# Linear attention, MoE and a second MLP on one core: the attention units from 10 on in one TensorE visit each, their k transposed on VectorE and through DRAM

## The chip, the core and the metric

One core of one Trainium2 chip runs the whole program. The metric is the device time of one execution in microseconds. The kernel before takes 721.27 us, the median of 3 runs (721.01 to 721.33). The engines are called by the names of the profile: PE is TensorE's matmuls and PEld its weight loads, DVE is VectorE, ACT is ScalarE, POOL is GpSimd, and SP is the engine whose queue issues nearly all DMAs.

## What is computed

Three layers, one after the other, on 3072 tokens (4 batches x 768) of 8 heads x 48 channels:

```python
for t in range(S):                       # attention, state [B, H, D, D], D = 48
    cur = einsum('bhd,bhe->bhde', u * k[t], v[t])
    y[:, :, t] = einsum('bhd,bhde->bhe', r[t], state + cur)
    state = w[t][..., None] * state + einsum('bhd,bhe->bhde', k[t], v[t])
x = y as [3072, 384]
h = x @ w_in                             # first MLP, 384 -> 2048 -> 384
x = (h * sigmoid(1.702 * h)) @ w_out
h = x @ w2_in                            # second MLP, 384 -> 1024 -> 384
s = h * softmax(h)
out = (s - mean(s)) / sqrt(var(s) + 1e-6) * g_ln @ w2_out
```

All is float32; the products of the MLPs are made of three matmuls each, on a high and a low part of either factor.

## The kernel before

**Units and blocks.** The tokens are cut into 24 attention units of 128 tokens (NU), each of two chunks of 64. The first MLP takes them in eight blocks of units, `BLOCKS`: three blocks of 2 units, two of 3 (blocks 3 and 4), three of 4 (blocks 5 to 7). A block runs in 16 steps, one for each 128 columns of the hidden layer. A step is `hstep` (line 597): `rise` (554), nine matmuls of the first layer into a PSUM bank `h` of which there are two; `gelu` (564), two ScalarE operations; and `rest` (572), one VectorE subtraction that makes the low part (the "gelu difference" below). `drain` (604) then runs `fall` (578), nine matmuls of the second layer, for the step two before. The columns of a matmul are the tokens of the block: 384 in blocks 3 and 4, 512 in blocks 5 and 6. After a block's last `fall`, `store` (590) copies the sums on ScalarE.

**Attention beside it.** While block j runs, the units of block j+1 are computed in the gaps. Up to about unit 9 the order of all engines is a list written out by hand, `START` (line 40). From unit 9 on, beside blocks 3 to 6, `steps_of` (716) says which of a unit's parts follow which step. Every engine runs its instructions in program order, and so does SP its DMAs: a DMA that waits holds all that stand behind it.

A unit i needs, on the way from load to output:
- `load_rkw` (105): r, k and the decay w by channel, 112 rows (48 channels of chunk 1, a gap, 48 channels of chunk 0), two buffers; `load_nat` (113): r and k by token; `load_v` (120) and `load_v2` (129).
- `f_scan` (135, forward products of w, VectorE), `f_r1` (141, GpSimd) and `f_r0` (147, VectorE), `f_back` (153: a small ScalarE copy `pc`, a reciprocal and the backward scan, line 159), `f_k` (162, the k product, line 166). They make scaled r and k.
- `bonus` (177, two GpSimd products), `bonus_sum` (184), `bonus_mul` (195, two GpSimd products of 64 rows, line 205), which leave the u term in `vd`.
- TensorE: `turn_k` (213, four transposes of k, line 217) with `copy_k` on ScalarE (219); `scores` (224, 16 small matmuls, lines 240 to 243 for units from 6 on), masked on VectorE (245, line 252); `states` (255, 16 small matmuls, lines 265 to 268), with `update` on VectorE (290, lines 305 and 308); `mix` (310, 32 small matmuls, lines 327 and 328), which makes y.
- `total` (330, adds y and `vd`), `send` (339, a 32x32-block transpose on VectorE and a DMA to DRAM), `fetch` (346, four DMAs back, so that y is transposed) and `out_hi`, `out_lo` (364, 374), which write the MLP's input.

**Visits.** In `steps_of` a unit is two visits of TensorE: `one` (727) has the transposes and scores of unit i+1 and the mix of unit i; `two` (758) has the states of unit i+1. Between them lie other steps. In a block of 3 units the visits follow steps 1, 6, 11 and 4, 9, 14; in one of 4 they follow steps 0, 4, 8, 12 and 2, 6, 10, 14. So units 9 to 11 run beside block 3, 12 to 15 beside block 4, 16 to 19 beside block 5 and 20 to 23 beside block 6. Where a block of 3 is followed by one of 4, the last unit (15) is `short`: its output goes through TensorE transposes (`turn`, 354, line 358) instead of DRAM.

**Queues.** On SP a unit's order is: rkw of unit i+3, v of i+2, the y write, four y reads (which wait for the write), v2, r and k by token.

Of the kernel before, what the change touches and what calls it, by code (L numbers as in the profile page):

```python
# [15 lines left out]
H, D, C = 8, 48, 64  # L16
HD = H * D
HC = H * C
# [5 lines left out]

QUADS = UB
DFF2 = NF2 * 128

# [39 lines left out]


def heads(ap, n=C):
    return ap.rearrange("p (h t) -> p h t", h=H)  # L70


class Attention:
# [31 lines left out]
    def load_rkw(self, i):  # L105
        if i < NU:
            rkw = self.get(i)["rkw"] = self.ap.tile([112, 2 * HC + H * PW + 2], F32, tag="rkw", name=f"rkw{i}", bufs=2)
            cut = 2 * HC if i < 2 else 0
            self.nc.sync.dma_start(out=rkw[:, cut:], in_=self.rkw[i, :, cut:])
            if cut:  # L110
                self.nc.sync.dma_start(out=rkw[:, 0:cut], in_=self.rkw[i, :, 0:cut])

# [55 lines left out]

    def front(self, i):
        if i < NU:  # L170
            self.f_scan(i)
            self.f_r1(i)
            self.f_r0(i)
            self.f_back(i)
            self.f_k(i)

    def bonus(self, i):
# [16 lines left out]

    def bonus_mul(self, i, e=None):
        nc, ap, s = self.nc, self.ap, self.st[i]
        dg = s["dg"]
        if e is not None:
            for h in range(H):
                v = s["vd"][:, h * D:(h + 1) * D]  # L200
                nc.scalar.activation(out=v, in_=v, func=AF.Copy, scale=dg[:, h:h + 1])
# [6 lines left out]
    def bonus_v(self, i):  # L208
        if i < NU:
            self.bonus_sum(i)  # L210
            self.bonus_mul(i)

# [42 lines left out]
    def states(self, i, chunk=None):  # L255
# [34 lines left out]
    def update(self, i, b, e=None):  # L290
# [7 lines left out]

        kv = self.bank(i, 3)[q:q + 48].rearrange("p (b c) -> p b c", b=2)[:, :, 0:4 * D]
        if b:  # L300
# [29 lines left out]
    def total(self, i, e=None):  # L330
        y, vd = self.st[i]["y"], self.st[i]["vd"]
        if i >= QUADS:
            vd = vd.rearrange("p (b c) -> p b c", b=2)
# [54 lines left out]
def rwkv_moe_moe2(ctx: ExitStack, tc: tile.TileContext, rkw, nat, vn, v2n, cst, w1, w2i, w2o, gln, out):  # L388
# [324 lines left out]
    at.dram = ctx.enter_context(tc.tile_pool(name="yd", bufs=2, space=bass.MemoryType.DRAM))  # L713
    at.spare = [x2b[:, (4 + k) * HD:(5 + k) * HD] for k in range(3)]

    def steps_of(j):

        S = [[] for _ in range(NF1)]  # L720
        u0, n = BLOCKS[j + 1]
        ones, twos = ((0, 4, 8, 12), (2, 6, 10, 14)) if n == 4 else ((1, 6, 11), (4, 9, 14))
        for i, a, b in zip(range(u0, u0 + n), ones, twos):
            nx, nn = i + 1 < NU, i + 2 < NU
            short = i + 1 == u0 + n and BLOCKS[j][1] < n

            def one(i=i, nx=nx, short=short):
                if nx:
                    at.turn_k(i + 1)
                    at.copy_k(i + 1)  # L730
                    at.scores(i + 1)
                at.mix(i)
                if nx:
                    at.load_rkw(i + 3)
                at.load_v(i + 2)
                at.total(i)
                if not short:
                    at.send(i)
                    at.fetch(i)
                if nx:  # L740
                    at.masked(i + 1, 0)
                    at.masked(i + 1, 1)

            def scan(i=i):
                at.f_scan(i + 2)
                at.f_r1(i + 2)

            def back(i=i):
                at.f_back(i + 2)

            def sums(i=i):
                at.bonus_sum(i + 1)

            def give(i=i):
                at.out_hi(i, X)
                at.out_lo(i, X)

            def two(i=i, nx=nx, short=short):
                if short:
                    at.turn(i)  # L760
                if nx:
                    at.states(i + 1)
                    at.load_v2(i + 2)
                if short:
                    give(i)
                if nx:
                    at.update(i + 1, 0)
                    at.update(i + 1, 1)
                    at.bonus_mul(i + 1)
                    at.load_nat(i + 3)  # L770
                    at.bonus(i + 2)

            def rest_of(i=i):
                at.f_k(i + 2)
                at.f_r0(i + 2)

            S[a] += [one]
            if nn:
                S[a + 1] += [scan]
            if nx:  # L780
                S[a if n == 4 else b - 1] += [sums]
            if nn:
                S[a + (1 if n == 4 else 2)] += [back]
            S[b] += [two]
            if not short:
                S[a + 3 if n == 4 else a + 4] += [give]
            if nn:
                S[b + 1] += [rest_of]
        return S

# [25 lines left out]
    with tc.manual_schedule():  # L816
        pend += [(2, NF1 - 2), (2, NF1 - 1)]
        for j in range(3, LAST):
# [116 lines left out]
def _layout(inp):  # L935
# [9 lines left out]

    rkw = np.zeros((NU, 112, 2 * HC + H * PW + 2), f)
# [6 lines left out]
    rkw[:, :, 2 * HC:-2] = wv.reshape(NU, 112, H * PW)  # L953

# [43 lines left out]
```

## Time and profile before

| | |
|---|---|
| median of 3 runs | 721.27 us (721.01 to 721.33) |
| profiled execution | 719.98 us, span 718.2 us |
| TensorE busy | 696.4 us (97%), clock granted 1.00 |
| VectorE busy | 548.2 us (76%) |
| ScalarE busy | 301.9 us (42%) |
| GpSimd busy | 167.0 us (23%) |
| blocks 3 to 6 | about 172 to 436 us of the span |

The span is what the profiler saw from the first to the last instruction; the execution's time is a little longer. A busy TensorE is read from starts: matmuls overlap, so the distance from one step's first matmul to the next step's is the step's cost. A group's idle time names what released it.

### The profile page before, as it was taken

Reading aid. Unit: us, or ns where it says so; the run is one execution under the profiler, and the core shown is the slowest. Engines: PE = TensorE matmul, PEld = TensorE weight load, DVE = VectorE, ACT = ScalarE, POOL = GpSimd, SP = SyncE. Lnnn points to the kernel's source line nnn. Section 1 sums busy time; section 2 is a strip of 40 time slices with the busy share of each in tenths; the row PEclk is TensorE's granted clock in tenths of the full one; section 3 lists DMA queues with packets and bytes.
Section 4 is the critical chain, followed back from the end, with each engine's and each line's share of the span. In section 5 each row is a group of like instructions: output and inputs, shape, how many; then the busy total and the mean of one; then the engine's idle time right before and its main releaser. Section 6 shows DMA issues by size and latency. Waiting matters only on the chain.

```text
span 718.2 us, 16290 instructions
## 1 busy us (share of the span) xinstructions
PE 696.4 (97%) x6596; PEld 619.3 (86%) x6596; DVE 548.2 (76%) x884; ACT 301.9 (42%) x604; POOL 167.0 (23%) x158
## 2 busy tenths in 40 slices
PE   2899999999999999999999999999999999999997
PEld 2679999999999999888888888888889989999997
DVE  8899999887767888866777632578588887788872
ACT  1465554333322322333223322465656545454552
POOL 5341222443333333423333300120000000000000
PEclk9999999999999999999999999999999999999999
DMA  8866624433333443333332103233135445444543
GB/s 252 271 189 216 219 80 113 120 100 89 104 95 97 127 128 97 95 95 100 101 91 56 34 23 103 80 103 89 59 117 180 152 140 180 144 140 144 161 155 103
DMA packets 53611, 88.77 MB, mean 124 GB/s; under 512 B 13632, under 2 KB 43200, under 8 KB 53536
## 3 DMA queue, kind: packets, MB, share of 16 engines
q1 hardware_dynamic: 53392, 87.63, 40.9%
q8 instruction: 52, 0.85, 0.5%
q14 instruction: 23, 0.19, 0.1%
q10 hardware_dynamic: 144, 0.10, 0.0%
HBM read 67.65 MB, written 20.05 MB: 122 GB/s over the span
## 4 chain that ended last, share of the span: by engine, by line
PE 92%; DVE 4%; ACT 2%; issue 1%; DMA 0%; ACTq 0%; DVEq 0%
PE acc L585 28%; PE h L560 26%; PE o L696 13%; PE right L628 8%; PE left L628 6%; PE att L327 2%; PE att L240 1%; PE att L217 1%; DVE P L138 1%; PE att L265 1%; PE att L328 1%; PE d L482 1%; DVE R L150 1%; PE att L358 1%; PE att L233 0%
## 5 line engine op out<-in xcount | busy, mean ns | idle before, releaser
L585 PE MATMUL acc<-gh,w 128*128 128x256 f32 (+2 forms) x768 | 212.4, 342 | 1.1 <-ACT x2a L595 0.8
L560 PE MATMUL h<-xTh,w 128*128 128x256 f32 (+2 forms) x768 | 173.9, 337 | 0.1
L568 ACT ACTIVATE gh<-h 128x256 fp32r<-128x256 f32 (+2 forms) x128 | 62.9, 491 | 244.5 <-PE h L560 236.2
L585 PEld LDWEIGHTS acc<-gh,w 128*128 128x128 f32 x768 | 136.5, 189 | 14.3 <-ACT x2a L595 1.1
L575 DVE TENSOR_TENSOR gl<-h,gh 128x256 fp32r<-128x256 f32 (+2 forms) x128 | 70.5, 553 | 90.2 <-ACT h L570 89.1
L560 PEld LDWEIGHTS h<-xTh,w 128*128 128x128 f32 x768 | 128.4, 189 | 12.3 <-ACT w L484 0.5
L585 PE MATMUL acc<-gl,w 128*128 128x256 f32 (+2 forms) x384 | 129.0, 336 | 0.0
L560 PE MATMUL h<-xTl,w 128*128 128x256 f32 (+2 forms) x384 | 87.6, 336 | 0.0
L585 PEld LDWEIGHTS acc<-gl,w 128*128 128x128 f32 x384 | 72.7, 189 | 5.3
L144 POOL TENSOR_TENSOR R<-rkw,P 64x512 f32<-64x512 f32 x24 | 32.1, 1336 | 185.3 <-issue 136.7
L696 PE MATMUL o<-w,qh 128*128 128x384 f32 x384 | 70.9, 336 | 0.0
L560 PEld LDWEIGHTS h<-xTl,w 128*128 128x128 f32 x384 | 64.7, 189 | 5.9 <-DVE xTl L378 0.2
L696 PEld LDWEIGHTS o<-w,qh 128*128 128x128 f32 x384 | 67.7, 188 | 1.6
L205 POOL TENSOR_TENSOR vd<-vs,dg 64x384 f32<-64x384 f32 x48 | 54.5, 1135 | 40.9 <-DVE dg L188 17.9
L570 ACT ACTIVATE h<-h 128x256 f32<-128x256 f32 (+2 forms) x128 | 62.5, 488 | 0.0
L673 POOL TENSOR_TENSOR sm<-sm,mhalf 128x1 f32<-128x1 f32 x24 | 13.2, 549 | 200.4 <-DVE sm L672 187.2
L159 DVE TENSOR_TENSOR_SCAN rkw<-rkw,ipc 112x520 f32<-112x520 f32 x24 | 41.6, 1731 | 0.8
L628 PE MATMUL right<-w,x2h 128*128 128x512 f32 x156 | 40.0, 392 | 0.9 <-ACT x2h L616 0.9
L181 POOL TENSOR_TENSOR nr<-nr,nk 128x384 f32<-128x384 f32 x24 | 27.7, 1155 | 43.3 <-DMA nk<-in_nat 42.1
L252 DVE TENSOR_TENSOR R<-att,cc 64x256 f32<-64x256 f32 (+1 forms) x82 | 36.7, 448 | 1.1
L696 PE MATMUL o<-w,ql 128*128 128x384 f32 x192 | 37.1, 334 | 0.0
L628 PEld LDWEIGHTS right<-w,x2h 128*128 128x128 f32 x156 | 29.1, 188 | 6.8 <-ACT x2h L616 1.2
(188 smaller groups left out, 1199.2 us busy)
## 6 DMA issues: line engine op xcount, KB each, us to landing
rkw<-in_rkw SPq DMA_DIRECT2D x22, 676.4 KB, 5.8
d<-t SPq DMA_DIRECT2D x24, 512.0 KB, 2.6
back<-d SPq DMA_DIRECT2D x96, 128.0 KB, 2.9
x2b<-in_w SPq DMA_DIRECT2D x11, 768.0 KB, 5.3
nr<-in_nat SPq DMA_DIRECT2D x24, 192.0 KB, 3.4
nk<-in_nat SPq DMA_DIRECT2D x24, 192.0 KB, 2.5
vs<-in_vn SPq DMA_DIRECT2D x48, 96.0 KB, 5.1
out<-ob SPq DMA_DIRECT2D x23, 192.0 KB, 2.2
```

The costliest lines, as they stand in the source:

```text
L144: (e or self.nc.gpsimd).tensor_tensor(out=heads(R1[0:64]), in0=heads(s["rkw"][0:64, 0:HC]), in1=heads(s["P"])[0:64, :, 0:C], op=ALU.mult)
L159: v.tensor_tensor_scan(out=w[:, n:0:-1], data0=w[:, n:0:-1], data1=self.ipc[:, n:0:-1], initial=0.0, op0=ALU.mult, op1=ALU.add)
L181: g.tensor_tensor(out=s["nr"], in0=s["nr"], in1=s["nk"], op=ALU.mult)
L205: nc.gpsimd.tensor_tensor(out=heads(vd[q:q + 64]), in0=heads(vt[q:q + 64]), in1=dg[q:q + 64].unsqueeze(2).to_broadcast([64, H, D]), op=ALU ...
L252: self.nc.vector.tensor_tensor(out=heads(R[q:q + 64])[:, h:h + n], in0=a, in1=m.unsqueeze(1).to_broadcast([64, n, C]), op=ALU.mult)
L560: nc.tensor.matmul(out=h_ps, lhsT=W1[f][:, ws + c * 128:ws + (c + 1) * 128], rhs=xs[:, c, tok], start=n == 0, stop=n == 8)
L568: nc.scalar.activation(out=gh, in_=h_ps, func=AF.Gelu_apprx_sigmoid)
L570: return nc.scalar.activation(out=h_ps, in_=h_ps, func=AF.Gelu_apprx_sigmoid)
L575: nc.vector.tensor_tensor(out=gl_, in0=g, in1=gh.bitcast(F32), op=ALU.subtract)
L585: nc.tensor.matmul(out=a, lhsT=W1[f][:, ws + e * 128:ws + (e + 1) * 128], rhs=gs, start=first and n == 0, stop=last and n == 2)
L628: nc.tensor.matmul(out=h_ps[:, b * 512:(b + 1) * 512], lhsT=xs[:, c], rhs=W2I[c][wb][:, b * 512:(b + 1) * 512], start=n == 0 and c == 0, s ...
L696: nc.tensor.matmul(out=o, lhsT=(lo if n == 2 else hi)[:, f * 128:(f + 1) * 128], rhs=W2O[f][n == 1], start=n == 0 and f == 0, stop=n == 2 ...
```

## The change

Units from `LONE` = 10 on are handled by a new table. `VISITS` gives the steps (counted from the start of block 3) after which units 9 to 23 have their one visit: 1, 6, 10, 14, 18, 22, 26, then every fourth from 32 to 60. Seven units (9 to 15) fall beside blocks 3 and 4, as before, but in other places. The lines of `ENTRY`, `SHORT` and `LONG` say what follows a visit's step, the next step, and so on; "+1" is the unit after the visit's.

- A visit holds scores and states of unit i+1 and the mix of unit i. For that, states go to the second half of their banks, and y to the bank that the transposed k had.
- k is no longer transposed on TensorE for units 11 to 23. `send_k` transposes it in 32x32 blocks on VectorE, writes it to DRAM and reads it back with four DMAs; `place_k` copies it on ScalarE, in two operations, where `copy_k` put it. For that the rkw load of these units has 128 rows, of which 16 are zero.
- `bonus_mul` is one GpSimd product of 128 rows on a `vd` that is loaded by a DMA of its own, instead of two of 64 rows.
- GpSimd's r product comes after the visit, beside bonus and the updates, and no longer right behind the forward scan.
- The short way of unit 15 is gone: all units go through DRAM. The y reads have one landing place instead of two; the third holds k.

```diff
+LONE = 10
+VISITS = (1, 6, 10, 14, 18, 22, 26) + tuple(range(32, 64, 4))
+ENTRY = (
+    "turn+1 copy+1 scores+1 mix rkw+3 v+2 total send vd+1 fetch masks+1",
+    "scan+2 back+2 k+2 sendk+2 r1+2 sum+1 mul+1 bonus+2",
+    "nat+3 r0+2",
+    "states+1 v2+2 updates+1 place+2 scan+3 back+3 k+3 sendk+3",
+    "hi lo",
+)
+SHORT = (
+    "scores+1 states+1 mix rkw+3 v+2 v2+2 total send vd+1 fetch masks+1",
+    "updates+1 r1+2 sum+1 bonus+2",
+    "mul+1 nat+3 place+2 r0+2 scan+3",
+    "back+3 k+3 sendk+3",
+    "hi lo",
+)
+LONG = (
+    "scores+1 states+1 mix rkw+3 v+2 v2+2 total send vd+1 fetch masks+1",
+    "r1+2 updates+1 sum+1 mul+1 bonus+2",
+    "r0+2 nat+3 place+2 scan+3",
+    "hi lo back+3 k+3 sendk+3",
+)
...
-            rkw = self.get(i)["rkw"] = self.ap.tile([112, 2 * HC + H * PW + 2], F32, tag="rkw", name=f"rkw{i}", bufs=2)
+            rkw = self.ap.tile([128, 2 * HC + H * PW + 2], F32, tag="rkw", name=f"rkw{i}", bufs=2)
+            s, n = self.get(i), 128 if i > LONE else 112
+            s["rkw"], s["rows"] = rkw[0:112], rkw
...
+        if i >= LONE:
+            nc.gpsimd.tensor_tensor(out=heads(s["vd"]), in0=heads(s["vd"]), in1=dg.unsqueeze(2).to_broadcast([128, H, D]), op=ALU.mult)
             return
...
+    def send_k(self, i):
+        s, K = self.st[i], self.spare[2]
+        kt = s["rows"][:, HC:2 * HC].rearrange("q (p h t) -> q h p t", p=4, h=4)
+        self.nc.vector.transpose(out=K.rearrange("q (h p t) -> q h p t", p=4, h=4), in_=kt)
+        d = self.dram.tile([128, HC], F32, tag="kd", name=f"kd{i}")
+        self.nc.sync.dma_start(out=d, in_=K)
+        d = d.rearrange("(r t) (h x) -> h t r x", r=4, h=4)
+        for h in range(4):
+            self.nc.sync.dma_start(out=K[32 * h:32 * h + 32].rearrange("t (r x) -> t r x", r=4), in_=d[h])
+
+    def place_k(self, i):
+        s, K = self.st[i], self.spare[2].rearrange("q (r p d) -> q p r d", r=4, p=4)
+        kTs = s["kTs"] = self.ap.tile([128, 4, 112], F32, tag="kTs", name=f"kTs{i}", bufs=1)
+        self.nc.scalar.activation(out=kTs[:, :, 0:96].rearrange("q p (r d) -> q p r d", r=3), in_=K[:, :, 0:3], func=AF.Copy)
+        self.nc.scalar.activation(out=kTs[:, :, 96:112], in_=K[:, :, 3, 0:16], func=AF.Copy)
...
-        Dx, Dy = s["D"] = self.bank(i, 2), self.bank(i, 0)
+        off = 4 * C if i >= LONE else 0
+        Dx, Dy = (self.bank(i, k)[:, off:off + 4 * D] for k in (2, 0))
...
-        if i < QUADS:
+        if i < QUADS or i >= LONE:
             s["y"] = y = self.bank(i, 1)[:, 0:HD]
...
-        back = self.spare[1 + i % 2]
+        back = self.spare[1]
...
-    def steps_of(j):
...
+    def steps():
...
+        G = [[] for _ in range(NF1 * (LAST - 3))]
+        for n, t in enumerate(VISITS):
+            for m, line in enumerate(ENTRY if n == 0 else SHORT if t < 2 * NF1 else LONG):
+                for op, _, i in (x.partition("+") for x in line.split()):
+                    i = LONE - 1 + n + int(i or 0)
+                    if i < NU:
+                        G[t + m].append(lambda op=ops[op], i=i: op(i))
+        return G
...
-            S = steps_of(j)
             for f in range(NF1):
                 hstep(j, f)
-                for g in S[f]:
+                for g in plan[16 * (j - 3) + f]:
                     g()
                 drain(2)
```

## Rows read from the trace of the kernel before

**Rows 1.** The page, part 4: the chain that ended last, by engine.

```profile
PE 92%; DVE 4%; ACT 2%; issue 1%; DMA 0%; ACTq 0%; DVEq 0%
```

**Rows 2.** Timeline, PE, block 5, a first visit: start us, us, line, operation, count.

```profile
350.08 0.84 PE L560 MATMUL h<-xTh,w 128*128 128x512 f32 x3
...
352.13 0.55 PE L217 MATMUL att<-cc,rkw 112*128 112x112 f32 x4
352.60 0.27 PE L240 MATMUL att<-R,rkw 48*64 48x64 f32 x1
...
356.23 0.85 PE L560 MATMUL h<-xTh,w 128*128 128x512 f32 x3
```

**Rows 3.** Timeline, PE, block 5, the second visit of the same period.

```profile
360.31 0.84 PE L560 MATMUL h<-xTh,w 128*128 128x512 f32 x3
...
362.45 0.24 PE L265 MATMUL att<-vs,kTs 64*48 64x48 f32 x1
...
362.95 0.50 PE L585 MATMUL acc<-gh,w 128*128 128x512 f32 x1
...
365.13 0.84 PE L560 MATMUL h<-xTh,w 128*128 128x512 f32 x3
```

**Rows 4.** Waits of PEld, 170 to 440 us: us in total, times, longest us.

```profile
PEld att L217 <- DVE rkw L166: 1.1, 2, 0.6
PEld acc L585 <- ACT x2a L595: 1.1, 2, 0.6
...
PEld acc L585 <- ACT x2b L595: 0.4, 1, 0.4
```

**Rows 5.** Timeline, PE, block 4: a plain step, then unit 15's transposes and states.

```profile
282.71 0.68 PE L560 MATMUL h<-xTh,w 128*128 128x384 f32 x3
...
285.83 0.68 PE L560 MATMUL h<-xTh,w 128*128 128x384 f32 x3
...
290.00 0.68 PE L560 MATMUL h<-xTh,w 128*128 128x384 f32 x3
```

**Rows 6.** Single lines on DVE: duration ns min/median/max, starts, forms.

```profile
L159 DVE TENSOR_TENSOR_SCAN rkw<-rkw,ipc x24: 1241/1856/2147, 5.4 to 400.4; 112x520 f32<-112x520 f32 x24
...
L342 DVE STREAM_TRANSPOSE x2b<-vd x14: 578/579/581, 179.4 to 431.6; 128x384 f32<-128x384 f32 x14
...
L656 DVE STREAM_TRANSPOSE t<-c x24: 1245/1246/1248, 506.5 to 698.7; 128x1024 f32<-128x1024 f32 x24
...
L308 DVE TENSOR_TENSOR vs<-P,pc x27: 552/679/1405, 173.9 to 422.8; 48x384 f32<-48x384 f32 x27
```

**Rows 7.** One period of block 4: us; busy PE, PEld, DVE, ACT, POOL; clock, DMA.

```profile
249.54:265.42 15.88, 15.53 (x205) 14.56 (x205) 13.53 (x21) 4.60 (x11) 6.17 (x5) 1.00 0.42 113
```

**Rows 8.** Timeline, POOL, the pair of bonus products beside a backward scan of block 4.

```profile
256.71 2.66 POOL L205 TENSOR_TENSOR vd<-vs,dg 64x384 f32<-64x384 f32 x2
```

**Rows 9.** SP: four y reads (timeline), and its waits for y writes, 172 to 300 us.

```profile
239.68 1.76 SPq L351 DMA_DIRECT2D x2b<-yd  x4
...
SPq L351 <- DMA yd<-x2b: 25.2, 6, 4.6
```

**Rows 10.** DMA issues in three stretches: count, KB each, median us from issue to landing.

```profile
rkw<-in_rkw SPq DMA_DIRECT2D x8, 676.4 KB, 5.9
...
x2a<-in_w SPq DMA_DIRECT2D x1, 768.0 KB, 4.3
...
yd<-x2b SPq DMA_DIRECT2D x1, 192.0 KB, 2.1
```

**Rows 11.** Lines by form, ACT, 172 to 300 us: count, busy us, mean ns, idle.

```profile
L372 ACT ACTIVATE xTh<-x2b 128x384 fp32r<-128x384 f32 x6 | 3.1, 510 | 0.0
```

**Rows 12.** Lines by form, DVE, 172 to 300 us.

```profile
L575 DVE TENSOR_TENSOR gl<-h,gh 128x384 fp32r<-128x384 f32 x32 | 17.7, 554 | 19.8 <-ACT h L570 19.2
...
L138 DVE TENSOR_TENSOR_SCAN P<-rkw,ind 112x520 f32<-112x520 f32 x7 | 8.6, 1230 | 0.0
...
L166 DVE TENSOR_TENSOR rkw<-rkw 112x512 f32<-112x512 f32 x8 | 5.7, 712 | 0.0
```

More of the change, by code (lines that the diff above doesn't have):

```diff
@@ L106, in load_rkw @@
         if i < NU:
-            rkw = self.get(i)["rkw"] = self.ap.tile([112, 2 * HC + H * PW + 2], F32, tag="rkw", name=f"rkw{i}", bufs=2)
+            rkw = self.ap.tile([128, 2 * HC + H * PW + 2], F32, tag="rkw", name=f"rkw{i}", bufs=2)
+            s, n = self.get(i), 128 if i > LONE else 112
+            s["rkw"], s["rows"] = rkw[0:112], rkw
             cut = 2 * HC if i < 2 else 0
-            self.nc.sync.dma_start(out=rkw[:, cut:], in_=self.rkw[i, :, cut:])
+            self.nc.sync.dma_start(out=rkw[0:n, cut:], in_=self.rkw[i, 0:n, cut:])
             if cut:
-                self.nc.sync.dma_start(out=rkw[:, 0:cut], in_=self.rkw[i, :, 0:cut])
+                self.nc.sync.dma_start(out=rkw[0:n, 0:cut], in_=self.rkw[i, 0:n, 0:cut])
     def load_nat(self, i):
@@ L167, in f_k @@
                                      in1=heads(s["rkw"][:, 2 * HC + 2:])[:, :, 0:C], op=ALU.mult)
[L169 to L175, printed above, removed]
     def bonus(self, i):
@@ L193, in load_vd, with bonus_mul @@
         self.nc.sync.dma_start(out=vd, in_=self.vn[i])
-    def bonus_mul(self, i, e=None):
+    def bonus_mul(self, i):
         nc, ap, s = self.nc, self.ap, self.st[i]
         dg = s["dg"]
[L198 to L201, printed above, removed]
+        if i >= LONE:
+            nc.gpsimd.tensor_tensor(out=heads(s["vd"]), in0=heads(s["vd"]), in1=dg.unsqueeze(2).to_broadcast([128, H, D]), op=ALU.mult)
             return
@@ L206, in bonus_mul @@
                                     in1=dg[q:q + 64].unsqueeze(2).to_broadcast([64, H, D]), op=ALU.mult)
[L208 to L211, printed above, removed]
     def turn_k(self, i):
@@ L297, in update @@
         src, dst = src.rearrange(pairs, a=4, b=2), dst.rearrange(pairs, a=4, b=2)
-        kv = self.bank(i, 3)[q:q + 48].rearrange("p (b c) -> p b c", b=2)[:, :, 0:4 * D]
+        kv = self.bank(i, 3)[q:q + 48].rearrange("p (b c) -> p b c", b=2)
+        off = 4 * C if i >= LONE else 0
+        kv = kv[:, :, off:off + 4 * D]
         if b:
@@ L331, in total @@
         y, vd = self.st[i]["y"], self.st[i]["vd"]
-        if i >= QUADS:
+        if QUADS <= i < LONE:
             vd = vd.rearrange("p (b c) -> p b c", b=2)
@@ L713, in rwkv_moe_moe2 @@
     at.dram = ctx.enter_context(tc.tile_pool(name="yd", bufs=2, space=bass.MemoryType.DRAM))
-    at.spare = [x2b[:, (4 + k) * HD:(5 + k) * HD] for k in range(3)]
-    def steps_of(j):
[L720 to L789, printed above, removed]
@@ new lines, in rwkv_moe_moe2, with masks, updates @@
+    at.spare = [x2b[:, a:a + n] for a, n in ((4 * HD, HD), (5 * HD, HD), (6 * HD, HC))]
+    def masks(i):
+        for b in range(2):
+            at.masked(i, b)
+    def updates(i):
+        for b in range(2):
+            at.update(i, b)
+    def steps():
+        ops = dict(
+            scores=at.scores, states=at.states, mix=at.mix, rkw=at.load_rkw, v=at.load_v, v2=at.load_v2, vd=at.load_vd, nat=at.load_nat,
+            total=at.total, send=at.send, fetch=at.fetch, hi=lambda i: at.out_hi(i, X), lo=lambda i: at.out_lo(i, X),
+            masks=masks, updates=updates, sum=at.bonus_sum, mul=at.bonus_mul, bonus=at.bonus, r0=at.f_r0, r1=at.f_r1,
+            scan=at.f_scan, back=at.f_back, k=at.f_k, sendk=at.send_k, place=at.place_k, turn=at.turn_k, copy=at.copy_k)
+        G = [[] for _ in range(NF1 * (LAST - 3))]
[6 more added lines that the diff above has]
+        return G
@@ L817, in rwkv_moe_moe2 @@
         pend += [(2, NF1 - 2), (2, NF1 - 1)]
+        plan = steps()
         for j in range(3, LAST):
-            S = steps_of(j)
             for f in range(NF1):
                 hstep(j, f)
-                for g in S[f]:
+                for g in plan[16 * (j - 3) + f]:
                     g()
@@ L944, in chan @@
         return a.reshape(B, H, UB, 2, C, D).transpose(0, 2, 3, 5, 1, 4).reshape(NU, 2, D, H, C)
-    rkw = np.zeros((NU, 112, 2 * HC + H * PW + 2), f)
+    rkw = np.zeros((NU, 128, 2 * HC + H * PW + 2), f)
     wv = np.zeros((NU, 112, H, PW), f)
@@ L952, in _layout @@
         wv[:, q:q + D, :, 1:] = chan(w)[:, ch]
-    rkw[:, :, 2 * HC:-2] = wv.reshape(NU, 112, H * PW)
+    rkw[:, 0:112, 2 * HC:-2] = wv.reshape(NU, 112, H * PW)
     def natural(a):
```

## The prediction

> **What bounds the kernel.** I read the page first: the chain that ended last is 92% TensorE [rows 1]. So a change pays by taking work or waits off TensorE's queue, and costs when another queue makes TensorE wait. Second, TensorE's timeline in one attention period of block 5 [rows 2, 3]. The same place of a step (its first xTh matmul) comes round after 4.08 us without attention (356.23 to 360.31), after 6.15 us with a first visit (350.08 to 356.23) and after 4.82 us with a second (360.31 to 365.13). The visits cost 2.07 and 0.74 us, 2.81 a unit. Third, TensorE's waits over blocks 3 to 6 [rows 4]: little, 2.6 us in three rows. Fourth, VectorE and the DMA queue, which are to carry the moved work [rows 6 to 10].
>
> **TensorE, what goes.** The four k transposes take from 352.13 to 352.60, 0.47 us [rows 2]. Without them the scores open the visit and pay the entry gap that the states pay now: the last xTl and xTh groups of a step leave 0.09 us before 362.45 [rows 3]. The states in the merged visit cost at most the 0.50 us from 362.45 to 362.95 [rows 3], and at least some 0.4, if the drain at their end, of the size of the entry gap, is shared. A merged visit is 2.07 - 0.47 + 0.09 + 0.4 to 0.5 = 2.1 to 2.2 us instead of 2.81: 0.62 to 0.72 a unit. I take 0.65, near the upper cost, because a gap between scores and states is new. It holds for units 11 to 23, thirteen (unit 10 is still transposed and has its states in a step of their own): **8.45 us**. Unit 15 loses its three output transposes: its step takes 4.17 us, against 3.12 without attention [rows 5] and 0.74 for states: **0.31 us**. The new place of y in another bank changes no instruction's shape: nothing.
>
> **TensorE, waits that go.** 1.1 us are transposes waiting for the k product on VectorE [rows 4]; k is now formed more than one period ahead of its scores. 1.5 us are the first second-layer matmuls of a block waiting for ScalarE to store the block before [rows 4], behind a small ScalarE copy that waits for the first scan; now scan and copy are a step apart. I take **2.6 us**; between 0 and 2.6, since ScalarE gets another waiting instruction, the placing of k.
>
> **VectorE.** One unit in block 4 is 15.88 us, of which VectorE works 13.53 [rows 7]. Added is a transpose of 128x512: 128x384 takes 0.58 and 128x1024 1.25 us [rows 6], so 0.71. The new period there is four steps of 3.12 and a visit, 14.6 us. With 14.24 VectorE would be at 97%. But the backward scan takes 1.24 us at best and 2.15 at worst [rows 6], and the worst stands beside GpSimd's pair of bonus products, 2.66 us [rows 8]. The new order puts GpSimd's work in the visit's step and the one or two after it, and the backward scan in the last step of the period, where GpSimd is done: up to 0.9 us come back. GpSimd itself saves one of the pair, 1.3 us. I take VectorE at 13.4 to 14.2 in 14.6, so no bound, and a step of delay is borne: the gelu difference of a step is first missed two steps later, some 2.8 us after it is usually done (three pieces of 1.56 us, less two gelu operations of some 0.5 each, like the copy in [rows 11], 0.55 of its own, and hand-overs).
>
> The Trainium skill, SBUF — State Buffer, section Who interferes with whom, says that GpSimd and a VectorE instruction with two SBUF inputs exclude each other, the loser for the whole of the other instruction. The rows agree in part: the update product takes 0.55 us at best and 1.41 at worst [rows 6], which is one GpSimd operation longer. What that would make of the time is the third rival.
>
> **ScalarE.** One copy of 448 columns becomes one of 384, 0.51 us [rows 11], and one of 64, which is above nothing and under those 0.51: at most half a microsecond a unit more, beside TensorE, on an engine that works 4.6 of 15.88 us [rows 7]. Its cost is its wait, below.
>
> **SP's queue and the round trip.** SP gets, a unit, one write of 256 KB, four reads of 64 KB and one load of vd. SP runs in order and waits where it stands: four reads now wait for the y write, 25.2 us in six units, and four issues take 1.76 us [rows 9]. The next rkw, v, v2 and y issues queue behind the k reads, so a loop is closed: rkw lands (L), forward scan 1.23, a gelu difference 0.55, backward scan 1.24 to 2.15, k product 0.71 (all [rows 6, 12]), transpose 0.71, k write lands (2.1, as a y write that had nothing ahead of it [rows 10]), four issues 1.76, next rkw. That is L + 8.3 to 9.2 us; it must stay under 14.6 in blocks 3 and 4, and under 18.5 in blocks 5 and 6. L is unknown: rkw grows from 112 to 128 rows. From above: 5.9 us [rows 10] times 8/7, 6.7. From below: a weight load of 128 rows and 768 KB landed in 4.3 [rows 10]. The new load is nearest to that one in rows and bytes, so I take 4.5 to 5: a loop of 12.8 to 14.2, just under the period, **0 us**.
>
> **New waits.** In the entry, unit 11's k is sent at step 2 and placed at step 4. Counted from the gelu difference of step 2: 4.8 to 5.7 us of VectorE, 2.1 for the write, 1.8 of issues, some 2 for the last read (as the write), 0.7 of placing, so 11.4 to 12.3; TensorE wants it after about 12.9 (three steps and 0.74, less the gelu's 1 us, two pieces of 1.56 and the scores). Cost 0, up to 3 us if the write takes as long as an rkw; I take 0.5. The gelu of step 5 stands behind that placing and is late by some 3 us, which the visit of step 6 covers. At the ends of blocks 4 and 5 the returns of units 15 and 19 come later, since their y write now stands behind the k reads and an rkw: with L at 4.3 they are in time, at 5.8 up to 1.2 us late, at 6.7 2 us. I take 0.5. The regular placing comes three steps after its sending, about as long as the trip takes; up to 2 us of waiting there only delay a gelu that has slack.
>
> **Sum.** 8.45 + 0.31 + 2.6 - 1.0 = 10.4 us. The profiled execution took 719.98 us, so 709.6; the median is 1.3 above it, so **710.9**. Bounds of this case: 13 x 0.72, all waits gone and none new give 12.3 (709.0); no old wait gone and 3 us new give 5.4 (715.9).
>
> **Rivals.**
> *The SP loop binds* in blocks 3 and 4. With L at 6.7 and the backward scan still at 2.15 it is 15.9, 1.3 over the period, five times between the visits of steps 6 and 26: 6.5, less the 2.8 of slack, 3.7 us, and 2 us for unit 19 instead of 0.5: 716.1. For it: the old rkw landed in 5.9 with fewer rows. Against it: the 768 KB load at 4.3.
> *Little is saved by merging*: scores, states and mix use different parts of the array and each change drains it. Then only transposes go, 0.38 x 13 + 0.31, with half the waits: 6.6, less 1, is 5.6: 715.7. Against it: now scores and mix stand in one visit, and states with entry and drain cost only 0.74.
> *VectorE becomes the bound, and the kernel slower.* If each of the four GpSimd instructions a unit (6.17 less half of the pair's 2.66, 4.8 us [rows 7, 8]) holds a VectorE instruction for its whole length, VectorE needs 13.53 + 0.71 - 1.2 (what the scan and the two update products lose now) + 4.8 = 17.8 against 14.6; 3.2 us over in each of six periods less 2.8 is 16.4 us: 710.9 + 16.4 = 727.3. It decides from 16.8 us a unit on (2.2 x 6 - 2.8 is the gain). For it: the 1.41. Against it: GpSimd's 6.2 us of work now cost VectorE only about 1.2 a unit [rows 6, 7].
> *The merge saves what the waits take*, and nothing can be measured: about 721.
>
> **Chances.** Forecast 0.60; SP loop 0.20, of which 0.14 remain faster, 0.04 the same and 0.02 slower; little saved 0.09; VectorE 0.09; even 0.02. A difference under 0.2% (1.4 us) is no change here. Faster 0.60 + 0.14 + 0.09 = 0.83; same 0.06; slower 0.11. The range begins at the forecast's best with a little to spare, 708.8, and reaches past the SP loop, to 717; the slower cases and the even one stay out.
>
> **What would show it.** Right: merged visits of 2.1 to 2.2 us each, no TensorE wait on k or a store, backward scans near 1.24, rkw landing by 5 us, SP idle before the k write. Wrong: states waiting for v2 or for placed k, gelu differences late in steps 10 to 31, the first matmuls of blocks 5 and 6 waiting for xT, SP issuing rkw later from visit to visit.

## The result and the profile after

The changed kernel takes **711.85 us**, the median of 4 runs (710.63 to 713.47), against 721.30 us of the kernel before beside it (721.01 to 722.65): a ratio of 0.9867, with a 95% interval from 0.9843 to 0.9891. The prediction was 710.9 us and faster. The sign and the time are right; two terms of the sum are not, and their errors lie on opposite sides. The profiled execution of after is the slowest of its four, 713.47 us with a span of 711.7.

**First the steps.** TensorE's timeline gives the distance from the first xTl matmul of a step to that of the next, so what a step costs with all that stands in it. Steps are counted from the first of block 3 (0) to the first of block 7 (64), as `VISITS` does. Before, this stretch takes 272.07 us, after 264.40: the gain is 7.67 us. What follows block 7's first step is 273.2 and 273.0 us. Ahead of block 3 the order of the work is as before, yet that step begins at 172.96 us before and at 174.30 after; over all executions shown here it begins between 172.69 and 175.13 us, and most of the difference is there by the first gelu, at 36.2 to 38.8 us, in a part of the program that the change leaves alone. This is scatter of the start. So the stretch is the sharper measure, and the experiments give it beside the time.

| us | before | after | k reads behind (e2) |
|---|---|---|---|
| step 36: first visit, or merged visit | 6.15 | 6.11 | 6.10 |
| step 38: second visit, or a plain step | 4.81 | 4.08 | 4.09 |
| step 37: plain | 4.08 | 4.08 | 4.08 |
| step 6: unit 11's entry | 5.16 | 5.56 | 5.67 |
| steps 16, 17, 21, 25 over those of e2 | | +0.28, +0.27, +0.20, +0.25 | 3.12 each |
| step 18 | 4.44 | 5.28 | 5.12 |
| steps 24, 28 | 5.79 each | 3.12, 3.13 | 3.12 each |
| steps 30, 31 (end of block 4) | 4.16, 3.30 | 4.85, 4.04 | 3.12, 3.30 |
| steps 34, 50 (a second visit before) | 5.23, 5.12 | 4.11, 4.12 | 4.10, 4.12 |
| step 47 (end of block 5) | 4.11 | 5.49 | 4.10 |
| **stretch, steps 0 to 63** | **272.07** | **264.40** | **259.46** |

**The merged visit costs 2.03 us**, 6.11 less 4.08, where the two visits cost 2.07 and 0.74 [rows 2, 3]. TensorE's timeline of after, block 5 (start us, us, line, operation, count), shows why:

```profile
345.79 0.61 PE L590 MATMUL h<-xTh,w 128*128 128x512 f32 x2
...
347.92 0.27 PE L267 MATMUL att<-R,rkw 48*64 48x64 f32 x1
...
348.40 0.22 PE L270 MATMUL att<-R,rkw 48*64 48x64 f32 x1
348.44 0.20 PE L294 MATMUL att<-vs,kTs 64*48 64x48 f32 x1
...
348.77 0.21 PE L296 MATMUL att<-v,kTs 64*48 64x48 f32 x1
348.90 0.23 PE L357 MATMUL att<-vs,R 112*32 112x48 f32 x1
...
351.89 0.62 PE L590 MATMUL h<-xTh,w 128*128 128x512 f32 x2
```

The first state stands 0.04 us behind the last score, as near as scores stand to each other. Between scores and states there is no gap; there is one between states and mix, 0.13 us from the start of the last state to that of the first mix, and one at the visit's entry.

**The waits.** Of the weight loads' waits from 165 to 435 us in after (us in total, times, longest), these answer to [rows 4]:

```profile
PEld h L590 <- DVE gl L605: 2.9, 5, 1.8
...
PEld h L590 <- ACT xTh L402: 1.5, 1, 1.5
...
PEld h L590 <- ACT gh L598: 0.8, 1, 0.8
...
PEld acc L615 <- ACT x2a L625: 0.2, 1, 0.2
PEld att L295 <- DMA v<-in_v2n: 0.2, 1, 0.2
```

No transposes wait for k any more, and the store of a block holds TensorE for 0.2 us instead of 1.5. New are waits for the gelu difference, for the MLP's input xTh and, once, for the gelu itself. Neither takes longer itself: the page's chain, by engine and by line, names what stands behind.

```profile
PE 85%; DMA 5%; DVE 5%; issue 2%; ACT 1%; SPq 1%; DVEq 0%; ACTq 0%
PE acc L615 24%; PE h L590 24%; PE o L726 14%; PE right L658 8%; PE left L658 6%; DMA rkw<-in_rkw 2%; PE att L357 2%; DMA yd<-x2b 1%; DMA x2b<-yd 1%; PE att L267 1%; DMA kd<-x2b 1%; DVE rkw L185 1%; PE att L358 1%; PE d L512 1%; DVE rkw L192 1%
```

TensorE's share has fallen from 92% [rows 1] to 85%, and DMA has gone from 0 to 5%, with rkw first and kd among it. **The chain from 249 to 266 us**, in order of time (start, us, what; small pieces and three of the four k read issues are left out here), shows how they hang together:

```profile
249.59 5.08 DMA rkw<-in_rkw
...
254.82 1.10 issue
255.92 0.53 DVE gl L605
256.45 0.12 DVE ipc L184
...
256.60 1.72 DVE rkw L185
...
258.34 1.50 DVE rkw L192
...
259.87 0.72 DVE x2b L238
...
260.61 2.00 DMA kd<-x2b
...
262.65 0.33 SPq L243
...
264.50 4.59 DMA rkw<-in_rkw
```

It goes from one rkw issue to the next, 14.91 us: landing, forward scan (the 1.10 told as issue), gelu difference, backward scan, k product, transpose, k write, and four k read issues with SP standing in between. That is the loop of the prediction's part on SP, and it is as long as it is because of two pieces. The backward scan takes 1.72 us, where 1.24 is its best, and the k product 1.50, where it was 0.71 [rows 6, 12]. GpSimd's timeline (idle before, and what ended it) says what stood beside them:

```profile
256.38 0.83 POOL L217 TENSOR_TENSOR vd<-vd,dg 128x384 f32<-128x384 f32 x1 [7.12 <-DMA vd<-in_vn]
257.25 2.03 POOL L170 TENSOR_TENSOR R<-rkw,P 64x512 f32<-64x512 f32 x1
...
272.01 1.80 POOL L170 TENSOR_TENSOR R<-rkw,P 64x512 f32<-64x512 f32 x1 [0.28 <-PE att L358]
```

GpSimd waits 7.12 us for vd, whose load stands in SP's queue behind the k reads and rkw, and its late bonus product meets the backward scan. The r product behind it then runs beside the scan and the k product. The r product's place is not vd's doing: its buffer comes free with the mix of TensorE's visit (L358), which ends at 257.12 us in this turn, and a turn later, at 272.01, it is that turn's mix that it waits for, with the bonus product done. It is the k product that comes late enough to meet it. Without the lengthening (0.48 and 0.79) the loop would be 13.64 us. The rkw issues of after are at 203.23, 219.42, 234.99, 249.59, 264.50 and 279.36: 76.13 us in five turns, 15.2 each, from 14.60 to 16.19. The longest, the first, is long by another piece: its k reads follow the k write's issue by 3.45 us (213.92 to 217.37). TensorE's period is 3 x 3.12 + 5.13 = 14.49.

### The profile page after: what moved, and what is told of

It reads as the page before. It is cut to its first block, busy times and chain, and to the rows that moved or that the text cites. A ratio compares the mean times of both kernels' runs of the same rounds, so it can differ in the third digit from the quotient of the medians.

```text
span 711.7 us, 16363 instructions
## 1 busy us (share of the span) xinstructions
PE 688.6 (97%) x6541; PEld 613.5 (86%) x6541; DVE 552.9 (78%) x898; ACT 304.0 (43%) x617; POOL 146.7 (21%) x144
## 4 chain that ended last, share of the span: by engine, by line
PE 85%; DMA 5%; DVE 5%; issue 2%; ACT 1%; SPq 1%; DVEq 0%; ACTq 0%
PE acc L615 24%; PE h L590 24%; PE o L726 14%; PE right L658 8%; PE left L658 6%; DMA rkw<-in_rkw 2%; PE att L357 2%; DMA yd<-x2b 1%; DMA x2b<-yd 1%; PE att L267 1%; DMA kd<-x2b 1%; DVE rkw L185 1%; PE att L358 1%; PE d L512 1%; DVE rkw L192 1%
## 5 line engine op out<-in xcount | busy, mean ns | idle before, releaser
L170 POOL TENSOR_TENSOR R<-rkw,P 64x512 f32<-64x512 f32 x24 | 33.8, 1410 | 87.7 <-PE att L358 43.5
L217 POOL TENSOR_TENSOR vd<-vd,dg 128x384 f32<-128x384 f32 x14 | 14.0, 999 | 116.8 <-DMA vd<-in_vn 61.4
L164 DVE TENSOR_TENSOR_SCAN P<-rkw,ind 112x520 f32<-112x520 f32 x24 | 32.0, 1335 | 7.5 <-DMA rkw<-in_rkw 7.3
L185 DVE TENSOR_TENSOR_SCAN rkw<-rkw,ipc 112x520 f32<-112x520 f32 x24 | 34.8, 1449 | 0.8
```

The costliest lines, as they stand in the source:

```text
L164: self.nc.vector.tensor_tensor_scan(out=P, data0=rkw[:, 2 * HC:2 * HC + H * PW], data1=self.ind[:, 0:H * PW], initial=0.0, op0=ALU.mult, o ...
L170: (e or self.nc.gpsimd).tensor_tensor(out=heads(R1[0:64]), in0=heads(s["rkw"][0:64, 0:HC]), in1=heads(s["P"])[0:64, :, 0:C], op=ALU.mult)
L185: v.tensor_tensor_scan(out=w[:, n:0:-1], data0=w[:, n:0:-1], data1=self.ipc[:, n:0:-1], initial=0.0, op0=ALU.mult, op1=ALU.add)
```

## The experiments

The theory after this reading: **SP's order closes a loop** (k write, k reads, next rkw, scan, k) that is a little longer than the period of blocks 3 and 4, and so costs what the merge would give. Rivals: the time is VectorE's or GpSimd's own; the merge saves little and the new waits are the entry's and the ends'. Each edit is against after, or against e2 where that is said; each kernel computes all of the reference.

**e1: after, unaltered.**

> The changed kernel unaltered, to see what of the first profile repeats. In that profile the stretch from the first step of block 3 to the first of block 7 fell from 272.1 to 264.4 us, and block 3 began 1.3 us later. Theory: the 7.7 us belong to the change and repeat within 1 us; the 1.3 us before block 3 do not, and the time is 710.5 to 712.5 us. Rival: the stretch itself varies from run to run by the 2.8 us that the four runs spread, because waits on DMAs decide there.

It took 712.83 us (711.68 to 713.85), 0.9879 [0.9865, 0.9894], with a stretch of 262.28 in its profile against 264.40. The waits are at the ends again, steps 30, 31 and 47, and within the blocks at 18, 25, 28 and 29, where after's profile has 16, 17, 18, 21 and 25, all in other sizes (47: 4.82 instead of 5.49). The theory's 1 us did not hold, the stretches differ by 2.12, and the time is 0.3 over its range; the rival is nearer. The rkw issues are 15.2 us apart here too (203.62 to 279.40 in five turns). A loop that is nearly as long as its period turns small differences into waits; so after has no single stretch.

**e2: the k reads behind the next rkw, v, v2, y write and vd.**

```diff
         self.nc.sync.dma_start(out=d, in_=K)
-        d = d.rearrange("(r t) (h x) -> h t r x", r=4, h=4)
+        s["kd"] = d
+
+    def fetch_k(self, i):
+        s, K = self.st[i], self.spare[2]
+        d = s["kd"].rearrange("(r t) (h x) -> h t r x", r=4, h=4)
         for h in range(4):
...
-    "scores+1 states+1 mix rkw+3 v+2 v2+2 total send vd+1 fetch masks+1",
+    "scores+1 states+1 mix rkw+3 v+2 v2+2 total send vd+1 fetchk+2 fetch masks+1",
```

> The four k reads are issued behind the next visit's rkw, v, v2, y write and vd, so that SP no longer stands waiting for the k write with rkw behind it. Theory (SP's order, k trip in front of the next rkw, makes the new waits of 5.6 us at the steps 6, 16 to 31 and 47): rkw lands before the forward scan wants it, the waits fall under 2 us, and the time is 707.5 to 709 us. Rival (VectorE and GpSimd hold each other up whatever SP does): the stretch stays within 1 us, 711 to 712.5 us. Third: the later k is now placed late and the states wait for it, 712 to 716 us.

**709.35 us** (707.78 to 709.62), 0.9826 [0.9809, 0.9842], and a stretch of 259.46, 4.9 us under after's and 2.8 under e1's. The time is 0.35 above the theory's range and outside the rivals'. Every step from 7 on is plain, and at the ends of blocks 4 and 5 nothing waits that did not wait before (step 31 has 3.30 in both). The rkw issues are 14.4 us apart (200.46 to 272.25 in five turns), about TensorE's pace. SP's timeline shows the next rkw right behind the k write, and the k reads waiting where nobody waits for SP:

```profile
242.95 0.33 SPq L240 DMA_DIRECT2D kd<-x2b  x1
243.32 1.13 SPq L135 DMA_DIRECT2D rkw<-in_rkw  x1
...
247.34 2.78 SPq L247 DMA_DIRECT2D x2b<-kd  x4
...
257.58 0.33 SPq L240 DMA_DIRECT2D kd<-x2b  x1
257.96 1.46 SPq L135 DMA_DIRECT2D rkw<-in_rkw  x1
```

The collisions with the backward scan and the k product went with the loop, although GpSimd's order was not touched: the k product is over at 256.80 us, and the r product, held by the mix as before, begins at 257.27. The bonus product now meets the forward scan instead (251.82, 1.76 us instead of 1.24), and no step waits for it. The backward scan and the k product from 200 to 290 us (duration ns min/median/max), first in after, then in e2:

```profile
L185 DVE TENSOR_TENSOR_SCAN rkw<-rkw,ipc x6: 1241/1742/1811, 210.7 to 287.7; 112x520 f32<-112x520 f32 x6
...
L192 DVE TENSOR_TENSOR rkw<-rkw x6: 691/1314/1505, 212.5 to 289.5; 112x512 f32<-112x512 f32 x6
```

```profile
L185 DVE TENSOR_TENSOR_SCAN rkw<-rkw,ipc x6: 1241/1242/1244, 211.5 to 283.2; 112x520 f32<-112x520 f32 x6
...
L192 DVE TENSOR_TENSOR rkw<-rkw x6: 691/692/693, 212.8 to 284.5; 112x512 f32<-112x512 f32 x6
```

**e3: the rkw load back to 112 rows,** and a second load of 16 rows for the k columns alone.

```diff
-            s, n = self.get(i), 128 if i > LONE else 112
+            s, n = self.get(i), 112
...
+            if i > LONE:
+                self.nc.sync.dma_start(out=rkw[112:128, HC:2 * HC], in_=self.rkw[i, 112:128, HC:2 * HC])
```

> rkw of the units from 11 on is loaded as 112 rows again, and the 16 zero rows of k by a second, small load. Theory (the row count that 16 engines share evenly by eights makes the load fast): the 112-row load lands in 5.5 to 6 us instead of 5.1, the loop through SP grows by about 1 us with the extra issue, the waits by 3 to 5 us, 714 to 717 us. Rival (bytes decide): it lands in about 4.6, and the time is 710 to 712 us.

715.17 us (714.47 to 716.69), 0.9915 [0.9900, 0.9930], stretch 266.95, which is 2.6 over after's and 4.7 over e1's. The same steps are late, more of them, and step 47 is at 6.09. The DMA issues from 172 to 300 us, first of after, then of e3 (count, KB each, median us to landing), show the larger load landing sooner:

```profile
rkw<-in_rkw SPq DMA_DIRECT2D x9, 773.0 KB, 5.1
```

```profile
rkw<-in_rkw SPq DMA_DIRECT2D x8, 676.4 KB, 5.5
...
rkw<-in_rkw SPq DMA_DIRECT2D x8, 32.0 KB, 5.5
```

0.4 us more of landing and one more issue, once a turn, cost 3.3 us by the medians: the loop is where the time hangs. The Trainium skill, SBUF — State Buffer, section Summary: rules for kernel authors, says to use 128 partitions in one DMA where a transfer binds; the two rows agree.

**e4: the states a step later, in a visit of their own.**

```diff
-    "scores+1 states+1 mix rkw+3 v+2 v2+2 total send vd+1 fetch masks+1",
-    "r1+2 updates+1 sum+1 mul+1 bonus+2",
+    "scores+1 mix rkw+3 v+2 total send vd+1 fetch masks+1",
+    "states+1 v2+2 r1+2 updates+1 sum+1 mul+1 bonus+2",
```

> The states leave the merged visit and are made after the next step, with v2's load behind them; k still goes through DRAM. Theory: a visit of scores and mix costs 2.07 - 0.47 + 0.09 = 1.7 us and one of states 0.74, so 0.4 us a unit more than the merged 2.03 that the trace shows, 13 x 0.4 = 5 us, partly covered because VectorE and SP get a longer period: 713 to 717 us. Rival (the entry gap is nothing and merging itself gains little): within 1 us of 711.9.

**729.55 us** (727.04 to 730.25), 1.0105 [1.0085, 1.0126], slower than before: neither expectation. In blocks 5 and 6 the price is plain, 1.68 and 0.73 us for the two visits against 2.03. But in blocks 3 and 4 steps of 7 to 8 us appear, and the first rows of these two timelines, of TensorE and of VectorE, say why:

```profile
203.95 0.21 PE L293 MATMUL att<-vs,kTs 64*48 64x48 f32 x1 [3.11 <-issue]
```

```profile
202.16 1.69 DVE L279 TENSOR_TENSOR R<-att,cc 64x256 f32<-64x256 f32 x4
```

States and scores share banks, as they did before the change (`Dx`, `Dy`; the change moved the states to the second half, `off`). Issued behind the masks, the states wait until VectorE has masked the scores, at 203.85, and VectorE's queue is several us behind. Then TensorE's clock falls after the idle time. Windows of 2 us of this stretch (busy us of PE, PEld, DVE, ACT and POOL, granted clock, DMA share, GB/s):

```profile
202.00:204.00 2.00, 0.05 (x4) 0.08 (x6) 1.93 (x6) 0.00 (x0) 0.00 (x0) 1.00 0.58 128
204.00:206.00 2.00, 2.00 (x40) 1.95 (x41) 1.79 (x4) 0.00 (x0) 0.00 (x0) 0.89 0.92 368
206.00:208.00 2.00, 2.00 (x8) 2.00 (x7) 0.32 (x1) 0.00 (x0) 0.00 (x0) 0.50 0.92 309
208.00:210.00 2.00, 2.00 (x11) 2.00 (x10) 0.00 (x0) 0.48 (x2) 0.83 (x1) 0.75 0.19 46
```

From 206 to 208 us it is at 0.50, the 1.2 GHz level, and three rise matmuls take 1.16 us instead of 0.68. So e4 mixes the price of a visit with a wait of its own; e5 takes the wait away.

**e5, on e2: the states in a visit of their own, and the masks behind them.**

```diff
-    "scores+1 states+1 mix rkw+3 v+2 v2+2 total send vd+1 fetchk+2 fetch masks+1",
-    "r1+2 updates+1 sum+1 mul+1 bonus+2",
+    "scores+1 mix rkw+3 v+2 total send vd+1 fetchk+2 fetch",
+    "states+1 v2+2 masks+1 r1+2 updates+1 sum+1 mul+1 bonus+2",
```

> As e2 (709.35 us), but the states of units 11 to 23 have a visit of their own in the step after the scores and mix, and the masks follow the states, so that the states wait for no mask. This prices the merging by itself. Theory A, the term of the prediction (0.65 a unit) and what the separated visits of blocks 5 and 6 showed in e4 (1.68 + 0.73 against 2.03, 0.38 a unit): 13 x 0.38 to 0.65 is 5 to 8.5, so 714 to 718. Theory B, the merged visit saves nothing and the gain is all in the transposes that are gone: 709 to 710. TensorE's waits stay at or below 2 us in either.

713.75 us (712.9 to 714.9), 0.9894 [0.9875, 0.9914], stretch 265.49, 6.03 over e2. A visit of scores and mix costs 1.68 us (5.76 less 4.08), the states' own 0.73: 2.41 against the merged 2.03. The merging by itself is worth **0.38 us a unit**, the lower end of theory A, in each unit from 12 on (unit 11's entry, steps 6 and 7, costs 1.5). The time is 0.25 under theory A's range, the stretch within its 5 to 8.5. Theory B falls.

**e6: k transposed on TensorE again, in a visit of its own, no trip.**

```diff
-    "r0+2 nat+3 place+2 scan+3",
-    "hi lo back+3 k+3 sendk+3",
+    "r0+2 nat+3 turn+2 copy+2 scan+3",
+    "hi lo back+3 k+3",
```

> The merged visit of after, but k is transposed on TensorE in a visit of its own, two steps after the merged one, copied by ScalarE, and neither VectorE's transpose nor the trip through DRAM is there. SP then has no k write and no k reads. Theory A (the transposes cost TensorE 0.47 us and an entry, 0.5 to 0.75 a unit, and the trip is what closes SP's loop): the waits at steps 16 to 31 and 47 go, and 13 x 0.5 to 0.75 is paid over e2: 716 to 719, slower than after by 4 to 7. Theory B (the waits of after come from something else, VectorE or GpSimd): the waits stay and the time is 718 to 722.

713.18 us (711.70 to 713.56), 0.9882 [0.9863, 0.9901], stretch 264.44. The waits at steps 16 to 31 and 47 are gone, as theory A had it, and thirteen steps are longer by 0.37 to 0.47 us for the transposes, less than the 0.5 to 0.75 expected. So the time is under the ranges of both theories, 2.8 under A's. TensorE's timeline shows one:

```profile
218.81 0.69 PE L590 MATMUL h<-xTh,w 128*128 128x384 f32 x3
219.34 0.55 PE L228 MATMUL att<-cc,rkw 112*128 112x112 f32 x4
219.66 0.42 PE L615 MATMUL acc<-gh,w 128*128 128x384 f32 x1
```

So with the k reads where the change put them, taking the transposes off TensorE has bought **little or nothing**: e6's stretch is after's to 0.04 us and 2.2 over e1's, and its time is 1.3 us above after's and 0.4 above e1's, with overlapping intervals. With the reads moved (e2) the same trip is worth 5.0 us of the stretch.

**e7, on e2: GpSimd's r product right behind the scan,** as before the change.

```diff
-    "r1+2 updates+1 sum+1 mul+1 bonus+2",
-    "r0+2 nat+3 place+2 scan+3",
+    "updates+1 sum+1 mul+1 bonus+2",
+    "r0+2 nat+3 place+2 scan+3 r1+3",
```

> As e2, but GpSimd forms the upper r product right behind the scan, as before the change, and so beside the backward scan or the k product. Theory A, the prediction's step on VectorE (GpSimd's new order keeps the backward scan at 1.24 us, and VectorE has little to spare in blocks 3 and 4): backward scans of 1.9 to 2.2 or k products of 1.5 us in most units, VectorE 0.8 us busier a unit, 1 to 4 us of new waits: 710 to 713. Theory B, VectorE has slack enough: the scans lengthen but TensorE waits no more than in e2, 709 to 710.

707.46 us (707.17 to 707.75), 0.9806 [0.9790, 0.9822], and a stretch of 259.44, e2's. The lower time lies in the start: block 3 begins at 172.99 us in this profile, at 175.13 in e2's. Neither theory is tested: the backward scan keeps its 1.24 us and the k product its 0.69, for the edit moved the line and not the work. The waits row of the r product (us in total, times, longest) shows it held until TensorE's mix of the next visit gives its buffer free:

```profile
POOL R L170 <- PE att L362: 69.2, 12, 12.3
```

**e8, on e2: the y write and y reads on ScalarE's queue.** The write (`send`) and the reads (`fetch`, a line later in the table) are issued with `nc.scalar.dma_start`.

```diff
-        self.nc.sync.dma_start(out=d, in_=t)
+        self.nc.scalar.dma_start(out=d, in_=t)
```

> As e2, but the y write and the four y reads are issued on ScalarE's queue, the reads one step later than the write. Theory: SP's order no longer binds in e2 but for the last turn of each block; taking y off it gives back at most the 0.2 of step 31 and 0.5 of step 6, so 708.5 to 709.5, the same as e2 within its scatter. Rival: five issues of some 0.4 us on ScalarE stand ahead of gelus and delay them, and ScalarE's wait for the y write holds back gelus: 710 to 714.

**727.30 us** (724.36 to 729.60), 1.0078 [1.0050, 1.0106]: the rival, and 13 us past its end. ScalarE's timeline and waits:

```profile
225.42 2.25 ACTq L385 DMA_DIRECT2D x2b<-yd  x4
227.72 0.49 ACT L602 ACTIVATE gh<-h 128x384 fp32r<-128x384 f32 x1 [6.49 <-DMA x2b<-yd]
...
ACT gh L602 <- DMA x2b<-yd: 36.7, 8, 6.5
ACT gh L602 <- DVE x2b L376: 22.8, 4, 6.4
```

The gelus stand behind an issue that waits for a DMA, or for VectorE's transpose; 6.5 us is more than the two steps that separate gelu and second layer.

**e9, on e2: GpSimd's bonus product asked for in the step of the backward scan.**

```diff
-    "r1+2 updates+1 sum+1 mul+1 bonus+2",
+    "r1+2 updates+1 sum+1 bonus+2",
...
-    "hi lo back+3 k+3 sendk+3",
+    "hi lo mul+1 back+3 k+3 sendk+3",
```

> As e2, but GpSimd's bonus product (0.8 us by itself) is asked for in the step of the backward scan, directly ahead of it, and so runs beside it; e7 could not move the r product there, because its third buffer comes free only at the next visit. Theory A, the prediction's step on VectorE: backward scans of 2.0 to 2.1 instead of 1.24, that is 0.8 us a unit more on an engine that the prediction put at 13.4 to 14.2 of 14.6 us; 1 to 4 us of new waits of TensorE in blocks 3 and 4 and the ends: 710 to 713. Theory B, e2 leaves VectorE enough room, and GpSimd's order is worth nothing: the scans lengthen and the steps stay as in e2: 707.5 to 709.6.

707.86 us (706.74 to 709.29), 0.9815 [0.9794, 0.9835], stretch 259.41: theory B's time, but again not its reason. GpSimd had nothing else to do and began the product when its data were there, beside the forward scan (251.73, both); the backward scan kept its 1.24 us. The rows are of GpSimd and of VectorE:

```profile
251.73 1.86 POOL L217 TENSOR_TENSOR vd<-vd,dg 128x384 f32<-128x384 f32 x1 [5.47 <-DVE R L176]
```

```profile
251.72 1.24 DVE L164 TENSOR_TENSOR_SCAN P<-rkw,ind 112x520 f32<-112x520 f32 x1
...
254.89 1.24 DVE L185 TENSOR_TENSOR_SCAN rkw<-rkw,ipc 112x520 f32<-112x520 f32 x1
```

What GpSimd's order is worth by itself thus stays open: two edits of the program's order did not change it on the chip.

**e10, on e2: the k reads right behind rkw, v and v2,** ahead of the y write, vd and the y reads.

```diff
-    "scores+1 states+1 mix rkw+3 v+2 v2+2 total send vd+1 fetchk+2 fetch masks+1",
+    "scores+1 states+1 mix rkw+3 v+2 v2+2 fetchk+2 total send vd+1 fetch masks+1",
```

> As e2, but the k reads stand right behind the next unit's rkw, v and v2, ahead of the y write, vd and the y reads. This tells which of the issues held back in after costs the time. Theory A (the loop k write, k reads, rkw, scan alone): the waits inside blocks 3 and 4 (steps 16 to 25) and at the ends of the blocks (30, 31 and 47) all go, 708 to 710 like e2. Theory B (the ends of the blocks wait for y, which stands behind the k reads, as the prediction's 0.5 us had it): steps 16 to 25 are plain, and 30, 31 and 47 keep 0.5 to 2 us each, 710 to 713.

708.85 us (707.17 to 709.15), 0.9820 [0.9800, 0.9840], stretch 259.32: theory A. Here y and vd stand behind the k reads, as in after, and nothing waits, at the ends neither. So it is the next unit's loads behind the k reads that cost the time, and the late y and late vd of after were late through them. rkw, v and v2 moved together here; that it is rkw is read from the chain, not tested by itself.

**e11: e2 again.**

> e2 unaltered. If the 2 us between e2 (709.35) and e7 (707.46) lie in the first 37 us of an execution alone, which hold only loads and the first layer, the stretch from block 3's first step to block 7's is again 259.4 to 259.6 us, and the time is anywhere from 707 to 710. If e7's edit had a worth, the stretch of e2 would be longer than e7's 259.44.

708.46 us (707.11 to 709.33), 0.9820 [0.9803, 0.9838], stretch 259.44. The five kernels with the k reads moved and the merged visit on SP's queue alone (e2, e7, e9, e10, e11: e7 and e9 do the same work at the same times) have medians from 707.46 to 709.35 and stretches within 0.14 us. They beat both kernels, after by 2.5 to 4.4 us.

## Why the prediction was right, and where it was wrong

**Merging, 8.45 us: right in kind, too small.** The saving is 2.81 less 2.03, 0.78 a unit, and 13 x 0.78 is 10.1. The transposes' part was right: predicted 0.47 less 0.09, 0.38; a visit of scores and mix alone costs 1.68 against 2.07, 0.39. The term that was mis-sized is the states in the merged visit, costed at 0.4 to 0.5 and taken near the upper end "because a gap between scores and states is new": they cost 2.03 less 1.68, 0.35, and no gap is there. The Trainium skill, TensorEngine Tiling (Array Packing), section Key Properties, has a rule for this that the prediction did not use: TensorE drains when the tiling mode changes, not when only the tile does. If 48x64 and 64x48 weights count as one mode, the trace agrees, with 0.04 us between scores and states and 0.13 before the mix with its weights 32 wide. No run varied a tile's size.

**Unit 15's turn, 0.31, and the old waits, 2.6: right.** Step 30 falls from 4.16 to 3.12 in e2, of which 0.73 is states: 0.31. The waits that go are 0.6 each at steps 18, 24 and 28, and 0.1 to 0.4 at 15, 16, 34 and 50: 2.8 us. The size is met; that it is the step between scan and copy that frees the store was not tested by itself. With e2's small remainders 10.1 + 2.8 + 0.3 - 0.5 is 12.7, and its stretch is 12.6 shorter than before's. That is the change without its queue: near the best case of the prediction, 12.3.

**SP's queue, 0 us: the step that failed.** The sum was L + 8.3 to 9.2 with L at 4.5 to 5, so 12.8 to 14.2, "just under the period". L came out at the upper end, 5.1 and 4.6 in the chain; in the turn shown the price of the k write (2.00), of the four issues (1.85) and of the transpose (0.72) was right too. VectorE's part, from the forward scan's start to the k write's issue, came out at 5.85 (254.76 to 260.61) instead of 4.4 to 5.3. The backward scan's 1.72 lies within the sum's 1.24 to 2.15; the k product was given its undisturbed 0.71 and took 1.50, and hand-overs were given nothing. The step that puts the backward scan "where GpSimd is done" left out that GpSimd's bonus product now waits for a DMA, vd, in that same queue: late rkw makes vd late, the late bonus product meets the backward scan, the late k product meets the r product that TensorE's mix releases, and each makes the next rkw later. With 15.2 us a turn against 14.49 the loop binds, in turns that are shorter than the rival's 15.9 on the average. The rival's chance was 0.20; in the mechanism what came is that rival, by another piece than L, and in size it is between the two. Of the prediction's own signs of being wrong, the gelu differences late within steps 10 to 31, the first matmuls of blocks 5 and 6 waiting and SP issuing rkw later from visit to visit all came.

**New waits, 1.0: too small by some 4 us.** Over the plain steps after's profile has 5.4 us: 0.4 at the entry, 1.2 within blocks 3 and 4, and 3.8 at the ends (1.73, 0.74 and 1.38 at steps 30, 31 and 47). The entry's 0.5 is right in size and not in reason: k is placed in time, at 195.65, and the states, from 196.5 on, wait for v2, 0.2 of the 0.4. The ends' 0.5 was argued from the y write standing behind k reads and rkw; e10 keeps that order and has no wait, so the lateness is the loop's, carried to the block's end.

**VectorE: right that it is no bound.** It works 13.50 and 13.68 us in two whole periods of e2 (239.64 to 254.12 and on to 268.61), of 14.49, as the 13.4 to 14.2 had it, and TensorE waits in neither. The third rival's 17.8 did not come. The lock that it rests on did: the Trainium skill, SBUF — State Buffer, section Who interferes with whom, has GpSimd and a VectorE instruction with two SBUF inputs exclude each other, and in after the k product beside GpSimd takes 1.50 instead of 0.69, while the r product takes 2.03 instead of the 1.17 to 1.19 of blocks 3 and 4 before. The r product ends 0.96 us after the backward scan that it met, and the k product 0.56 after the r product, each a little less than it takes alone, as if each had waited for the other to end. The meeting cost time by lengthening a loop, not by filling the engine.

**The sum.** Merging +1.6 and old waits +0.2 over the terms, new waits 4.4 under: 10.4 should have been 7.8 in this execution, and the stretch says 7.67. By the medians the gain is 9.45, as e1's stretch (9.79) would have it: the time of 710.9 was met to 0.95 us in part by luck, because a merge that was sized too low and a loop that was sized too short lie on opposite sides.

## What to carry to other kernels

In a queue that runs in order, follow every new wait round to itself: sum the loop from an issue to the same issue of the next turn, with the lengthened durations of instructions that meet another engine's, and compare it with the period; when it comes near (here 14.2 was forecast against 14.6), move the waiting issue behind those that start the next turn. An engine whose input comes to depend on that queue is part of the loop, also when it is idle half the time. And a line moved in the program moves the work only if something ahead of it on its engine, or its data, holds it there: read the trace of the edit before reading its time.

## What was not expected of the hardware

- The first 37 us of an execution scatter by up to 2.4 us (block 3's first step at 172.69 to 175.13 us), with kernels that are alike there. Two medians that differ by 2 us need not differ in the changed code; the distance between two steps held to 0.14 us over five kernels.
- A load of 112 rows and 676 KB lands later (5.5 us) than one of 128 rows and 773 KB (5.1).
- In e4 TensorE was half busy from 198 to 200 us (0.99 of 2.00), busy to 200.84 and then idle for 3.1 us. The granted clock was 1.00 up to 205 us, a microsecond after work had begun again at 203.95, then fell to 0.50, the 1.2 GHz level, from 206 to 208, and was back at 1.00 from 210 us on.
- Four transposes that stand by themselves between two steps cost 0.37 to 0.47 us, hardly more than the 0.39 they cost within a visit.
